# A last product in seven block products, accumulated in halves of PSUM banks, and its weights converted one stage later

## The chip, the cores and the metric

The kernel runs on one core of a Trainium2 chip. The time is device microseconds (us) of one execution. The engines are named as in the profile: PE is TensorE's matrix multiply and PEld its weight loads, DVE is VectorE, ACT is ScalarE, POOL is GpSimd, and SP is the queue that issues nearly all DMAs here.

## What is computed

The reference is a chain: windowed attention, then two stacks of matrix products. Cut to what matters:

```python
x = attention(q, k, v)                      # 4 x 8 heads x 576 x 64, window 64 -> x: 2304 x 512
a = x @ w1; b = x @ w2                      # 512 -> 1024
x = (a * b) @ w3 @ w_out                    # 1024 -> 1024 -> 512, "y" in the kernel
h = x @ w_in                                # 512 -> 2048
g = np.maximum(0.01 * h, h)                 # leaky relu
out = g @ w_out2                            # 2048 -> 512, float32
```

The weights arrive as 64-bit floats and are handed over as 64-bit integers; the kernel makes 32-bit floats of their words itself.

## The kernel before

Every large product is done three times on PE: each operand is split into a high and a low part in a rounded 32-bit type, and `mm3` (lines 74 to 77) issues high by high, high by low and low by high. Lines L75, L76 and L77 of the profile are these three matmuls, whatever stage they belong to; a stage is known by the tile's name.

The stages follow each other:

- **w3 with w_out** are multiplied into one matrix `wf` while the weights land (tiles `mm<-w,w3T`), together with the first batch's attention.
- **x to y**, four batches of 16 steps. `ab_step` multiplies x by w1 and w2 (tiles `ab`, 288 columns), `y_step` multiplies the product by `wf` (tiles `mm`, 288 columns). The next batch's attention is laid between (`sc` are its scores, `pa` its second product, which takes `pts`, loaded back from a DRAM tile `pd`). Here too the words of w_in (16 units) and w_out2 (16 units) are converted: `advance` (lines 284 to 314) takes a unit of 128 by 512 values that a DMA has landed in `raw`, scales the high words on ACT (L293, `f`), takes three bits of the low words on ACT (L295, `low`), shifts and joins them on DVE (L310) and sets the sign on DVE (L306); `keep` stores the result to the DRAM tile `wd`. The loads of units wait, by an order edge, for the last entry of `pss["store"]`, which `tp` sets to the store of `pd`. One call of `advance` is made per step, from step 4 of the second batch on (line 692).
- **y to h** is done in seven block products instead of eight: y and w_in are cut in quarters, `y_parts` and `w_parts` form sums of quarters and split them, and a `Quad` (p, c) multiplies the seven pairs for 256 of the 2048 columns (p, 0 to 7) and 768 of the 2304 rows (c, 0 to 2): tiles `pr`, 384 columns, 42 matmuls in a quad. ACT copies products out of PSUM (L640) and DVE adds others to them (L643), in the order that `Quad.ORDER` gives; the result `c` goes to the DRAM tile `hd`. `at_slot` lays the preparation of operands to slots, and a slot is one of the seven products (6 matmuls).
- **h to out**, the last stage, is a plain product: for each chunk c of 384 rows and each f of 16 blocks of 128 columns, `load_h` fetches a piece of h, `split_h` makes the leaky relu (ACT L748 and DVE L749) and the two parts (ACT L750 and DVE L751), and `o_step` multiplies three blocks of 128 rows by 128 rows of w_out2 (tiles `o`, 512 columns; 9 matmuls to a step). The rows of w_out2 come back from `wd` and are split by `store` (L259 and L260). One PSUM bank holds one block of 128 rows until all 16 steps have been added.

Of the kernel before, what the change touches and what calls it, by code (L numbers as in the profile page):

```python
# [21 lines left out]
def tile_kernel(ctx: ExitStack, tc: tile.TileContext, q, k, v, w1, w2, w3, w_out, w_in, w_out2, out):  # L22
# [184 lines left out]
    def tp(g):  # L207
# [75 lines left out]

    def advance(stop):

        now = dict(n_of)
        if now["scale"] < min(stop, now["load"]):
            u = units[now["scale"]]
            w = flat(u["raw"]).bitcast(I32).rearrange("p (m two) -> p m two", two=2)
            u["hi"] = w[:, :, 1]  # L290
            u["f"] = stage.tile([P, UC], F32, name="f", tag="f", bufs=4)
            with tc.issue_after(pss["copy"]) if now["scale"] >= PHASE_B else nullcontext():
                act.mul(u["f"], u["hi"].bitcast(F32), 2.0 ** -112)  # L293
                u["low"] = stage.tile([P, UC], I32, name="low", tag="low", bufs=1)
                act.activation(out=u["low"], in_=flat(u["raw"]).bitcast(U8).rearrange("p (m e) -> p m e", e=8)[:, :, 3],  # L295
                               func=AF.Copy, scale=1.0 / 32, bias=-31.0 / 64)
# [10 lines left out]
        if now["shift"] < now["scale"]:  # L307
            u2 = units[now["shift"]]
            g = u2["f"].bitcast(I32)
            dve.scalar_tensor_tensor(out=g, in0=g, scalar=3, in1=u2["low"], op0=ALU.logical_shift_left, op1=ALU.bitwise_or)  # L310
            n_of["shift"] += 1
        if d:
            n_of["bits"] += 1
# [70 lines left out]
    for f in range(KF2):  # L384
        unit(w_out2[P * f:P * f + P, :], keep(KF2 + f), ("wo2", f))
    n_of["cap"] = len(units)
# [181 lines left out]
    def w_parts(p):  # L568
# [4 lines left out]
        def part(j):  # L573
            u = win[p]
            a11, a21, a12, a22 = u[0][:, :, 0], u[0][:, :, 1], u[1][:, :, 0], u[1][:, :, 1]
            if j == 1:
                if p:
                    both = stage.tile([P, 2, 2, 2, P], F32, name="raw", tag="raw", bufs=RAW)
                    own["sums"] = [both[:, 0], both[:, 1]]
                else:  # L580
                    own["sums"] = [stage.tile([P, 2, 2, P], F32, name="io", tag="io", bufs=2) for _ in range(2)]
# [306 lines left out]
```

## Time and profile before

| what | value |
|---|---|
| median of 3 runs | 868.76 us (868.71 to 870.02) |
| profiled execution, its own time | 870.25 us |
| its span, first to last instruction | 868.5 us |
| PE busy in the span | 820.0 us (94%) |
| DVE, ACT busy | 513.9 us (59%), 438.8 us (51%) |
| last stage, first to last matmul of `o` | 662 to 862 us |

The profiled execution has 1.75 us around its span. PE's busy time counts modelled ends of pipelined matmuls; the distance from one matmul's start to the next says more than a matmul's duration.

### The profile page before, as it was taken

The page shows a single profiled execution, that of the slowest core. Times are in us where ns is not written, and L with a number is a line of the kernel's source. Part 1 is how long each engine was busy: PE and PEld are TensorE (multiplying, and loading weights), DVE is VectorE, ACT ScalarE, POOL GpSimd, SP SyncE. Part 2 cuts the span into 40 slices and gives each one's busy share as a digit, 9 for nine tenths or more (in the row PEclk, how much of TensorE's full clock was granted, in tenths as well). Part 3 has the DMA queues.
Part 4 walks back from the last instruction along what each step waited for, and adds up shares of the span by engine and source line. Part 5 has one row for each costly group of instructions (what it writes and reads, how often), then busy time and mean ns, then how long its engine had stood idle before and what let it go on. Part 6 is the DMA issues. An engine that isn't in the chain of part 4 may idle for free.

```text
span 868.5 us, 15320 instructions
## 1 busy us (share of the span) xinstructions
PE 820.0 (94%) x5332; PEld 754.7 (87%) x5332; DVE 513.9 (59%) x1307; ACT 438.8 (51%) x1091; POOL 66.7 (8%) x77
## 2 busy tenths in 40 slices
PE   5788798999999899899999999999998999999997
PEld 4567698989999899899999999999997888888885
DVE  6897996563676567564821864433338555555552
ACT  6676983432555365454521654333336555455552
POOL 1012543110111001110000000000000000000000
PEclk9999999999999999999999999999999999999999
DMA  7797787664688888875610355333239335344341
GB/s 249 197 209 205 203 212 199 140 152 88 162 216 215 213 251 220 234 240 160 184 46 1 128 188 193 133 134 135 105 121 290 102 98 166 94 134 130 99 129 45
DMA packets 203694, 139.44 MB, mean 161 GB/s; under 512 B 137312, under 2 KB 181856, under 8 KB 203616
## 3 DMA queue, kind: packets, MB, share of 16 engines
q1 hardware_dynamic: 199008, 133.74, 54.2%
q10 hardware_dynamic: 4608, 4.72, 1.6%
q8 instruction: 42, 0.69, 0.3%
q14 instruction: 36, 0.29, 0.1%
HBM read 94.63 MB, written 43.78 MB: 159 GB/s over the span
## 4 chain that ended last, share of the span: by engine, by line
PE 73%; DMA 12%; ACT 5%; DVE 4%; SPq 3%; issue 2%; POOL 1%; ACTq 0%; DVEq 0%; POOLq 0%
PE o L75 8%; PE o L76 8%; PE o L77 8%; PE pr L75 6%; PE pr L77 6%; PE pr L76 6%; PE ab L75 6%; PE ab L77 6%; DMA raw<-in_moe_w_dram 6%; PE ab L76 6%; PE mm L75 3%; PE mm L77 3%; PE mm L76 3%; DMA pts<-pd 2%; PE sc L175 2%
## 5 line engine op out<-in xcount | busy, mean ns | idle before, releaser
L75 PE MATMUL ab<-x,w 128*128 128x288 f32 x512 | 154.6, 302 | 6.1 <-ACT x L235 3.3
L77 PE MATMUL ab<-x,w 128*128 128x288 f32 x512 | 152.5, 298 | 0.0
L76 PE MATMUL ab<-x,w 128*128 128x288 f32 x512 | 152.3, 298 | 0.0
L75 PE MATMUL o<-w,g 128*128 128x512 f32 x288 | 113.2, 393 | 2.9 <-DVE c L643 2.9
L76 PE MATMUL o<-w,g 128*128 128x512 f32 x288 | 113.1, 393 | 0.0
L75 PE MATMUL pr<-yop,w 128*128 128x384 f32 x324 | 109.3, 337 | 1.4 <-ACT c L640 1.4
L77 PE MATMUL pr<-yop,w 128*128 128x384 f32 x324 | 109.1, 337 | 0.0
L76 PE MATMUL pr<-yop,w 128*128 128x384 f32 x324 | 109.0, 336 | 0.0
L75 PEld LDWEIGHTS ab<-x,w 128*128 128x128 f32 x512 | 97.7, 191 | 7.8 <-ACT x L235 3.5
L77 PEld LDWEIGHTS ab<-x,w 128*128 128x128 f32 x512 | 97.4, 190 | 0.1
L76 PEld LDWEIGHTS ab<-x,w 128*128 128x128 f32 x512 | 97.4, 190 | 0.1
L640 ACT COPY c<-pr 128x384 f32<-128x384 f32 x95 | 45.6, 480 | 94.5 <-PE pr L77 89.8
L643 DVE TENSOR_TENSOR c<-pr,c 128x384 f32<-128x384 f32 x74 | 41.1, 556 | 78.2 <-PE pr L77 59.6
L77 PE MATMUL o<-w,g 128*128 128x512 f32 x288 | 82.8, 393 | 0.0
L749 DVE TENSOR_TENSOR t<-h,t 128x384 f32<-128x384 f32 x96 | 53.5, 557 | 48.5 <-ACT t L748 48.4
L748 ACT ACTIVATE t<-h 128x384 f32<-128x384 f32 x96 | 50.4, 525 | 53.2 <-DVE g L751 52.5
L75 PE MATMUL mm<-ab,wf 128*128 128x288 f32 x256 | 76.8, 312 | 0.0
L77 PE MATMUL mm<-ab,wf 128*128 128x288 f32 x256 | 74.8, 294 | 0.0
L76 PE MATMUL mm<-ab,wf 128*128 128x288 f32 x256 | 74.4, 293 | 0.0
L751 DVE TENSOR_TENSOR g<-t,g 128x384 fp32r<-128x384 f32 x96 | 53.4, 557 | 29.7 <-ACT g L750 29.2
L183 ACT ACTIVATE s<-s,nm 128x128 f32<-128x128 f32 x144 | 56.5, 396 | 24.0 <-DVE nm L179 23.6
L75 PEld LDWEIGHTS o<-w,g 128*128 128x128 f32 x288 | 54.1, 188 | 15.4 <-DVE c L643 3.3
(94 smaller groups left out, 1560.8 us busy)
## 6 DMA issues: line engine op xcount, KB each, us to landing
hd<-c SPq DMA_DIRECT2D x96, 192.0 KB, 1.9
h<-hd SPq DMA_DIRECT2D x96, 192.0 KB, 2.4
raw<-in_moe_w_dram SPq DMA_DIRECT2D x32, 512.0 KB, 4.8
raw<-in_moe_w_out_dram SPq DMA_DIRECT2D x24, 512.0 KB, 4.5
raw<-in_moe_w_in_dram SPq DMA_DIRECT2D x16, 512.0 KB, 5.3
wd<-f SPq DMA_DIRECT2D x32, 256.0 KB, 4.1
vt<-in_v_dram SPq DMA_DIRECT2D x56, 128.0 KB, 2.7
pd<-tb SPq DMA_DIRECT2D x36, 192.0 KB, 2.3
```

The source lines that it names most:

```text
L75: pe.matmul(ps, lhsT=lh, rhs=rh, start=first, stop=False, skip_group_check=more)
L76: pe.matmul(ps, lhsT=lh, rhs=rl, start=False, stop=False, skip_group_check=more)
L77: return pe.matmul(ps, lhsT=ll, rhs=rh, start=False, stop=last, skip_group_check=more).ins
L175: pe.matmul(sc[:, t, :], lhsT=qb[:, t, :], rhs=kT[n][:, k0:k0 + P], start=True, stop=True)
L183: act.activation(out=s[:, t, :], in_=s[:, t, :], func=AF.Exp, bias=nm[:, t:t + 1], scale=-1.0, accum_out=sm[:, t:t + 1])
L640: pss["copy"] = act.copy(self.sb[to], ps).ins
L643: pss["add"] = dve.tensor_tensor(out=self.sb[to], in0=self.ps[at], in1=self.sb[of or to], op=ALU.add).ins
L748: act.mul(t, h, 0.01)
L749: dve.tensor_tensor(out=t, in0=h, in1=t, op=ALU.max)
L751: dve.tensor_tensor(out=g[:, 1], in0=t, in1=f32(g[:, 0]), op=ALU.subtract)
```

## The change

The last stage becomes seven block products too. The names w_out2's operands now go by are `v_load`, `v_parts` and `vop`; those of h are `h_load`, `h_sums`, `h_split` and `g_units`. A group is 512 rows (four groups, and a last one of 256), and k is one of 8 blocks of 256 columns of h. A step (group, k) has two `o_quad`s of 21 matmuls of 256 columns (one in the last group). All 8 steps of a group add into the same PSUM tiles: `BANKS` gives the products of one quad as four banks, two products to a bank in its halves, except one. After step 7 `o_out` adds the seven products to the four quarters of the result. The leaky relu is one ACT instruction (L814), in place on 128 by 1024 values. The last three p of y to h now run c by c, so that the operands of y come free earlier, and the first operands of the last stage are made in their room.

w_out2's words are converted beside y to h (`c_load`, `c_scale`, `c_shift`, `c_sign`, at slots 38 to 122), and only w_in's in the batches, from step 4 of the third batch on. For these the ACT instruction for `low` is gone: DVE shifts and masks, and joins the three bits straight from the low word in one instruction more. `pss["store"]` is now the last load of `pts`. The operands of w_in are one tile of seven for each p. The diff, cut to its core:

```diff
@@ tp, advance
-        pss["store"] = sp.dma_start(pd, tb).ins
+        sp.dma_start(pd, tb)
...
-            sp.dma_start(pts[32 * b:32 * b + 32], pd[:, b].rearrange("(a j) t i -> j a (t i)", a=4))
+            pss["store"] = sp.dma_start(pts[32 * b:32 * b + 32], pd[:, b].rearrange("(a j) t i -> j a (t i)", a=4)).ins
...
+                if now["scale"] < PHASE_B:
+                    low_bits(u)
...
+            if "low" in u2:
+                dve.scalar_tensor_tensor(out=g, in0=g, scalar=3, in1=u2["low"], op0=ALU.logical_shift_left, op1=ALU.bitwise_or)
+            else:
+                dve.tensor_scalar(g, g, 3, 0x7FFFFFF8, op0=ALU.logical_shift_left, op1=ALU.bitwise_and)
...
+            if "low" not in u:
+                dve.scalar_tensor_tensor(out=f, in0=u["lo"], scalar=29, in1=f, op0=ALU.logical_shift_right, op1=ALU.bitwise_or)
...
-            if 2 * KF * b + s >= 2 * KF * (B - 3) + 4:
-                advance(len(units))
+            if 2 * KF * b + s >= 2 * KF * (B - 2) + 4:
+                advance(KEPT)
@@ last stage
-    def o_step(c, f):
-        g = g_t.pop((c, f))
-        w = rows2(slots["wo2", f // 2])
-        for tb in range(TB):
-            if f == 0:
-                po[c, tb] = ps3.tile([P, DM], F32, name="o")
-            ts = slice(P * tb, P * tb + P)
-            mm3(po[c, tb], g[:, 0, ts], g[:, 1, ts], w[:, 0, f % 2, :], w[:, 1, f % 2, :], f == 0, f == KF2 - 1)
...
+    BANKS = ((1, 2), (6, 7), (4, 5), (3,))
...
+            for at, x in (((0, u[:, 0, 0:1]), (1, u[:, 1])), ((3, own.get("sums", (0,))[0]),), ((5, own.get("sums", (0, 0))[-1]),))[j]:
+                w = slice(at, at + x.shape[1])
+                act.copy(t[:, 0, w], x)
+                dve.tensor_tensor(out=t[:, 1, w], in0=x, in1=f32(t[:, 0, w]), op=ALU.subtract)
...
+            act.activation(out=x, in_=x, func=AF.Prelu, alpha=0.01)
+            x = hin[i] = x.rearrange("p f (t m) -> p (f t) m", t=2)
+            t13, t24 = hsum[i] = [stage.tile([P, 2, width(i)], F32, name="f", tag="f", bufs=4) for _ in range(2)]
+            dve.tensor_tensor(out=t13, in0=x[:, 1:4:2], in1=x[:, 0:2], op=ALU.subtract)
+            dve.tensor_tensor(out=t24[:, 0], in0=x[:, 3], in1=t13[:, 0], op=ALU.subtract)
+            dve.tensor_tensor(out=t24[:, 1], in0=x[:, 2], in1=t24[:, 0], op=ALU.subtract)
...
+            for at, y in ((0, x[:, 0:1]), (1, x[:, 2:4]), (3, t13), (5, t24)):
+                h, l = (u[:, n, at:at + y.shape[1], 0:width(i)] for n in range(2))
+                act.copy(h, y)
+                dve.tensor_tensor(out=l, in0=y, in1=f32(h), op=ALU.subtract)
...
+        if k == 0:
+            po[g, q] = [ps3.tile([P, 2, 2 * P], F32, name="o") for _ in BANKS]
+        for bank, ms in enumerate(BANKS):
+            for n, m in enumerate(ms):
+                a, b = O_PRODUCTS[m]
+                with tc.issue_after(pss["pr"]):
+                    pss["pr"] = mm3(po[g, q][bank][:, n], y[:, 0, b, ts], y[:, 1, b, ts], w[:, 0, a], w[:, 1, a],
+                                    k == 0 and n == 0, k == NF - 1, True)
...
+        act.copy(own, m1)
+        add(res[:, 0, lo], m2, own)
+        add(u2, m6, own)
+        add(u3, m7, u2)
+        add(u2, m45[:, 1], u2)
+        add(res[:, :, hi], m45, u3.unsqueeze(1).to_broadcast([P, 2, 2 * P]))
...
+        add(res[:, 1, lo], m3, u2)
...
-    order = [(p, c) for c in range(NP) for p in range(FIRST)] + [(p, c) for p in range(FIRST, NF) for c in range(NP)]
+    LAST_P = range(NF - 3, NF)
+    order = ([(p, c) for c in range(NP) for p in range(FIRST)] + [(p, c) for p in range(FIRST, NF - 3) for c in range(NP)]
+             + [(p, c) for c in range(NP) for p in LAST_P])
...
+    for f in range(KF2):
+        t0 = 38 + 5 * f
+        for n, g in ((0, c_load), (7, c_scale), (8, c_shift), (9, c_sign)):
+            at_slot(t0 + n, lambda f=f, g=g: g(f))
...
+        h_load(i + 4)
+        h_sums(i + 3)
+        for q in range(width(i) // P):
+            o_quad(i, q)
+        h_split(i + 2)
+        if i < len(later):
+            if i % 2 == 0 and i:
+                v_load(5 + i // 2)
+            run(later[i])
```

`later` holds the parts of `v_parts` for k = 5, 6 and 7; those for k = 0 to 4 are laid to slots of y to h.

How the instructions stand on PE where y to h ends and the last stage begins (`pr` is a product of y to h, `o` of the last stage; `yop` is y's or, in the last stage, the room of y's operands). Before:

```order
3559 L77 MATMUL pr<-yop_6577,w_7623 128x384
3560 L75 MATMUL o<-w_7897,g 128x512
3561 L76 MATMUL o<-w_7897,g 128x512
3562 L77 MATMUL o<-w_7897,g 128x512
3563 L75 MATMUL o<-w_7897,g 128x512
```

With the change:

```order
3559 L77 MATMUL pr<-yop_6414,w 128x384
3560 L75 MATMUL o<-yop 128x256
3561 L76 MATMUL o<-yop 128x256
3562 L77 MATMUL o<-yop 128x256
3563 L75 MATMUL o<-yop 128x256
```

The matmuls of the last stage start at the same place, have half the columns, and read both operands from the room of y's operands.

DVE early in the last stage. Before, the leaky relu's maximum (L749) and the split (L751) alternate, and nothing else stands there:

```order
1030 L749 TENSOR_TENSOR t<-h,t 128x384
1031 L751 TENSOR_TENSOR g<-t,g 128x384
1032 L749 TENSOR_TENSOR t<-h,t 128x384
1033 L751 TENSOR_TENSOR g<-t,g 128x384
```

With the change, in the first group (L817 to L819 are `h_sums`, L829 `h_split`, L788 and L792 `v_parts`; `yop`, `yop_7863` and `yop_8080` are now rooms of the last stage's operands):

```order
1129 L817 TENSOR_TENSOR f<-raw 128x512
1130 L829 TENSOR_TENSOR yop_7863<-raw,yop_7863 128x512
1131 L788 TENSOR_TENSOR io<-raw 128x256 x2
1132 L792 TENSOR_TENSOR yop_8080<-raw,yop_8080 128x256
1133 L792 TENSOR_TENSOR yop_8080<-raw,yop_8080 128x512
1134 L818 TENSOR_TENSOR f<-raw,f 128x256
1135 L788 TENSOR_TENSOR io<-io,raw 128x256
1136 L829 TENSOR_TENSOR yop_8080<-raw,yop_8080 128x256
1137 L829 TENSOR_TENSOR yop_8080<-f,yop_8080 128x512
1138 L819 TENSOR_TENSOR f<-raw,f 128x256
1139 L788 TENSOR_TENSOR io<-raw,io 128x256
```

The sums and splits of h and those of w_out2 are woven into each other on one queue.

SP in the second batch of x to y, where loads of attention and of units share the queue. Before:

```order
162 L279 DMA raw<-in_moe_w_in_dram 128x2x256 x2
163 L378 DMA wd<-f 128x512
164 L151 DMA qin<-in_q_dram 32x18x32 x4
165 L216 DMA pts<-pd 32x4x96 x4
166 L213 DMA pd<-tb 128x384
167 L279 DMA raw<-in_moe_w_in_dram 128x2x256
```

With the change, at such a place:

```order
143 L151 DMA kin<-in_k_dram 32x18x32 x4
144 L213 DMA pd<-tb 128x384
145 L216 DMA pts<-pd 32x4x96 x4
146 L151 DMA vt<-in_v_dram 128x4x64 x4
147 L213 DMA pd<-tb 128x384
148 L151 DMA qin<-in_q_dram 32x18x32 x3
```

The loads and stores of units are gone from the second batch; those of w_in stand in the third and fourth.

## Rows read from the trace of the kernel before

**Rows 1.** The page: PE's granted clock in 40 equal slices, tenths of full speed.
```profile
PEclk9999999999999999999999999999999999999999
```

**Rows 2.** Busy time and matmuls of each stage: three batches of x to y, y to h, last stage.
```profile
core 0: us, PE busy (x) PEld busy (x) DVE busy (x) ACT busy (x) POOL busy (x), PEclk, DMA share, GB/s
...
150.00:233.00 83.00, 81.60 (x711) 78.65 (x710) 46.21 (x177) 33.44 (x124) 9.94 (x12) 1.00 0.55 126
233.00:316.00 83.00, 79.29 (x671) 76.50 (x670) 52.62 (x171) 41.70 (x124) 7.53 (x9) 0.98 0.83 221
316.00:399.00 83.00, 79.99 (x688) 77.32 (x688) 53.14 (x182) 44.54 (x140) 9.25 (x11) 1.00 0.82 232
...
482.00:662.00 180.00, 176.30 (x1005) 175.34 (x1003) 92.48 (x184) 79.59 (x170) 0.00 (x0) 1.00 0.46 156
662.00:862.00 200.00, 199.34 (x864) 162.37 (x864) 110.69 (x200) 104.00 (x204) 0.00 (x0) 1.00 0.40 119
```

**Rows 3.** The same view in stretches where PE has matmuls of 288, 384, 512 columns alone.
```profile
450.00:482.00 32.00, 32.00 (x242) 32.00 (x241) 6.00 (x14) 6.54 (x17) 0.00 (x0) 1.00 0.04 11
500.00:640.00 140.00, 140.00 (x802) 140.00 (x801) 61.69 (x123) 53.61 (x113) 0.00 (x0) 1.00 0.42 146
702.00:730.00 28.00, 28.00 (x121) 22.55 (x120) 15.20 (x29) 15.38 (x30) 0.00 (x0) 1.00 0.40 117
```

**Rows 4.** 128-column matmuls of PE: durations (min/median/max ns), then timeline (start, us).
```profile
L175 PE MATMUL sc<-kT,qbd x30: 271/275/377, 211.0 to 234.6; 128*128 128x128 f32 x30
...
216.38 0.83 PE L175 MATMUL sc<-kT,qbd 128*128 128x128 f32 x6
```

**Rows 5.** Groups by line with shapes: weight loads of the last stage, then ACT's conversions.
```profile
L75 PEld LDWEIGHTS o<-w,g 128*128 128x128 f32 x288 | 54.1, 188 | 15.4 <-DVE c L643 3.3
...
L293 ACT ACTIVATE f<-raw 128x512 f32<-128x512 f32 x72 | 48.8, 677 | 25.5 <-DMA raw<-in_moe_w_dram 18.1 <-DMA raw<-in_moe_w_out_dram 3.5 <-DMA raw<-in_moe_w_in_dram 1.7
...
L589 ACT CAST w<-raw 128x512 fp32r<-128x512 f32 x21 | 12.8, 622 | 0.1
...
L589 ACT CAST w<-raw 128x256 fp32r<-128x256 f32 x7 | 2.9, 409 | 0.6 <-ACT io L514 0.6
```

**Rows 6.** Timeline of DVE at the start of y to h, one behind the other.
```profile
485.80 0.42 DVE L590 TENSOR_TENSOR w<-raw,w 128x256 fp32r<-128x256 f32 x1
486.13 0.88 DVE L585 TENSOR_TENSOR raw<-raw 128x256 f32<-128x256 f32 x2
486.93 0.68 DVE L590 TENSOR_TENSOR w<-raw,w 128x512 fp32r<-128x512 f32 x1
487.53 1.02 DVE L546 TENSOR_TENSOR yop<-f,yop 128x384 fp32r<-128x384 f32 x2
```

**Rows 7.** Wait of PE from 640 to 664 us: total, times, longest.
```profile
PE o L75 <- DVE c L643: 2.9, 1, 2.9
```

**Rows 8.** Chain of work that ended last, 285 to 305 us: start, us, what.
```profile
293.42 2.27 SPq L151
...
297.80 1.95 DMA pts<-pd
...
301.40 0.24 PE ab L76
...
304.00 0.13 PE mm L77
```

**Rows 9.** Timeline of the tail: DVE's last copies: start, us, what, idle time before.
```profile
862.05 0.75 DVE L770 COPY io<-o 128x256 f32<-128x256 f32 x2 [5.16 <-ACT io L769]
865.06 0.42 DVE L770 COPY io<-o 128x256 f32<-128x256 f32 x1 [2.26 <-ACT io L769]
```

**Rows 10.** Timeline of DVE in the last stage, with its waits for ACT.
```profile
700.39 0.56 DVE L751 TENSOR_TENSOR g<-t,g 128x384 fp32r<-128x384 f32 x1 [0.40 <-ACT g L750]
701.54 0.56 DVE L749 TENSOR_TENSOR t<-h,t 128x384 f32<-128x384 f32 x1 [0.59 <-ACT t L748]
```

**Rows 11.** A DMA group: queue, count, KB of each, median us to landing.
```profile
raw<-in_moe_w_out_dram SPq DMA_DIRECT2D x24, 512.0 KB, 4.5
```

More of the change, by code (lines that the diff above doesn't have):

```diff
@@ L383, in tile_kernel @@
                  keep(2 * p + h), ("win", p, h))
-    for f in range(KF2):
-        unit(w_out2[P * f:P * f + P, :], keep(KF2 + f), ("wo2", f))
-    n_of["cap"] = len(units)
+    n_of["cap"] = KEPT = len(units)
     for name, p in [("wo", i) for i in range(4)] + [(n, p) for p in range(2) for n in ("w1", "w2")] + [("wf", i) for i in range(4)]:
@@ L576, in part @@
             if j == 1:
[L577 to L581, printed above, removed]
+                own["sums"] = [stage.tile([P, 2, 2, P], F32, name="io", tag="io", bufs=2) for _ in range(2)]
             if j in (1, 2):
@@ L661, in step @@
                     self.add("c21", "b")
+                if m == 5:
+                    self.sb["c12"] = self.sb["c22"]
+                    self.room("c22")
+                    self.add("c22", "b", "c12")
+                    self.out("c22")
                 if m == 4:
@@ new lines, in tile_kernel, with c_load, c_scale @@
+    BANKS = ((1, 2), (6, 7), (4, 5), (3,))
+    GTOK = 512
+    GROUPS = [(t0, min(GTOK, T - t0)) for t0 in range(0, T, GTOK)]
+    steps = [(g, k) for g in range(len(GROUPS)) for k in range(NF)]
+    conv = {}
+    def c_load(f):
+        u = conv[f] = {"raw": stage.tile([P, UC], I64, name="raw", tag="raw", bufs=RAW)}
+        sp.dma_start(u["raw"], w_out2[P * f:P * f + P, :])
+    def c_scale(f):
+        u = conv[f]
+        u["hi"] = u["raw"].bitcast(I32).rearrange("p (m two) -> p m two", two=2)[:, :, 1]
+        u["f"] = stage.tile([P, UC], F32, name="f", tag="f", bufs=4)
+        act.mul(u["f"], u["hi"].bitcast(F32), 2.0 ** -112)
+        low_bits(u)
@@ L838, in tile_kernel @@
             done += 1
[L839 to L848 removed]
+    while done <= max(todo, default=0):
+        prepare(done)
+        done += 1
+    yw.release()
     ps2.release()
     ps_h.release()
[L851 removed]
+    po_out = tc.alloc_tile_pool(name="po_out", bufs=2, side="right", reuse_waits="tile")
     ps3 = tc.alloc_tile_pool(name="ps3", bufs=8, space=PSUM, reuse_waits="tile")
[L853 to L856 removed]
+    later = []
+    for k, tile in ((5, w_unit), (6, next_unit), (7, next_unit)):
+        a, b, c = v_parts(k, tile)
+        later += [(a,), (b, c)]
+    h_load(2)
+    v_load(5)
+    h_load(3)
+    for i in range(len(steps)):
+        if i == 0:
+            three(ph, "yop2")
+            g_units.append(spare.pop())
+            h_sums(2)
+        h_load(i + 4)
[7 more added lines that the diff above has]
+            run(later[i])
+    for p in (ps3, po_out, yb0, ph, stage):
         p.release()
```

202 lines of the change are left out of this document (116 added, 86 removed).

## The prediction

> **What bounds the kernel now.** I read the granted clock first: full speed in all 40 slices, the stretch of rows 8 being too short to show there [rows 1]. Then the busy times by stage [rows 2]. The reader is to see that PE is the bound in all of them: in y to h it is busy 176.3 of 180 us, in the last stage 199.3 of 200, while DVE is busy 110.7 and ACT 104.0 there. So a stage's time is its number of matmuls times the distance between their starts. That distance comes from stretches with one width alone [rows 3]: 32 us / 242 = 132 ns at 288 columns, 140 / 802 = 175 at 384, 28 / 121 = 231 at 512. The matmuls last longer than that, but overlap.
>
> Where PE is not full: batches two and three of x to y (79.3 and 80.0 of 83 us against 81.6 in the first, which converts no units [rows 2]), 2.9 us at the start of the last stage, where PE waits for an add of DVE [rows 7], and the tail. In batch two one case can be followed in the chain [rows 8]: SP takes 2.27 us to issue an attention load, the `pts` loads come behind it, and after the wait PE's 288-column matmuls are 0.24 us apart instead of 0.13 from about 300 to 303 us. The granted clock of 0.98 in this batch [rows 2] says that this is the lower of its two levels, 1.2 instead of 2.4 GHz, after PE had stood idle.
>
> **The last stage, by PE.** Before: 864 matmuls of 512 columns, 200.0 us [rows 2]. After: 9 quads of 128 rows, 8 k, 7 products, 3 matmuls each: 1512 of 256 columns. The trace has no such width. A straight line through 288 and 512 columns gives 132 - 32 x (231 - 132) / 224 = 118 ns [rows 3]. Bounds: from above the 288-column row, 132; from below the 128-column row [rows 4], six in 0.83 us of which the last takes 0.275 itself, so (0.83 - 0.275) / 5 = 111. I take 118, since 256 is next to 288 and the rows up to 512 lie on one line. 1512 x 118 = 178.4 us: **-21.6 us** (-32.2 at 111, -0.4 at 132).
>
> Weight loads go from 864 to 1512, and one lasts 188 ns [rows 5]. That doesn't add up to 284 us, because loads overlap: in the 288-column stretch 241 of them are done in 32.0 us, one in 133 ns [rows 3], and at 128 columns load and matmul together take 111 [rows 4].
>
> The Trainium skill, Perfetto Trace Analysis, "Identifying the Most-Contended Engine", judges TensorE's headroom by the busy share of LDWEIGHTS rather than by that of matmuls; by that this change would be bound by loads and lose. The 288-column stretch speaks against it: loads are busy all of it, at 133 ns each, and PE keeps its pace. The skill, TensorE: Matmul & The Clock Gate, "Back-to-back issue gap", gives N / 2.4 + 2.5 ns, an estimate of 109 ns for 256 columns, and with it 165 us for the stage, 13.6 less than my term; but at 288 and 512 columns it gives 122.5 and 216, and this trace has 132 and 231.
>
> **The last stage, by DVE and ACT.** From one start to the next DVE takes 0.33 us for 256 elements and 0.60 for 512 [rows 6]. A step has `h_sums` 0.60 + 2 x 0.33 and `h_split` 0.33 + 3 x 0.60: 3.39 us, while PE takes 42 x 0.118 = 4.96. `o_out` is 5 x 0.33 + 0.60 = 2.25 a quad. A group: 8 x 3.39 + 2 x 2.25 = 31.6 against PE's 39.6. The first group also makes w_out2's operands for three k (4 x 0.33 + 0.33 + 3 x 0.60 = 3.45 each): 42.0, which is 2.4 more than PE. ACT: L814 on 1024 elements isn't in the trace; two L293 of 512, 1.35 us, bound it from above [rows 5], and I take that. With casts of 0.41 + 3 x 0.62 [rows 5] a step has 3.6 us, which is less than PE's, so the leaky relu costs nothing; without PE's 4.96 over it, it would cost the 1.35.
>
> Splits run two steps ahead, 9.9 us, which covers the 2.4 if the two queues keep busy. `o_out` frees banks one by one while the other quad's 21 matmuls (2.5 us) run; its chain takes about as long. I take **+3 us** for both (0 to +8).
>
> **Conversion beside y to h.** 16 units, each 2 x 0.67 us of ACT [rows 5] and, at DVE's 0.60, 1.2 of DVE: 21 and 19 us, under 180 us in which ACT is busy 79.6 and DVE 92.5 [rows 2]. SP gets 16 loads of 512 KB, landing in 4.5 us [rows 11], and 16 stores; the 12.6 MB in some 95 us come to 130 GB/s on top of 156, near 290, more than the 221 and 232 of batches two and three [rows 2]. Behind them on SP wait the stores of `hd`, which hold the buffers `c`, and for those ACT's copies and then PE. Toward its end the stage also makes the first operands of the last stage: five k of w_out2 (17 us of DVE) and two steps of h (7 us). I take **+1.5 us** (0 to +6).
>
> **Batches.** Batch two loses its units: it goes from 79.3 to the first batch's 81.6 busy us, 2.3, and the stretch at half clock is gone, about 14 matmuls x 0.11 = 1.5 [rows 2, 8]. Batch three keeps 16 units, with one DVE instruction more and one ACT instruction less on each (9.6 us of DVE on 53.1 of 83 busy), and `pts` ahead of a unit's load; I give it +0.3. **-3.5 us** (-5.5 to +2).
>
> **Start and tail of the last stage.** The first quad still needs banks that DVE's last adds free, with a full DVE queue: 2.9 us as now, **0** (-2.9 to +3). At the end the last copy of DVE ends at 865.48 and the span at 868.5 [rows 9]: 3.0 us for the store. After the last matmul there will be one add of 512 (0.68), one of 256 (0.42) and some 0.4 until they begin, then the 3.0: 4.5 instead of 6.5, **-1.9 us** (-3 to +1).
>
> **Sum**, against the profiled execution's 870.25 us: -21.6 + 3 + 1.5 - 3.5 + 0 - 1.9 = -22.5, so 847.75. The median of the runs is 1.5 below that execution (868.76), so 846.
>
> **Rivals.**
> *DVE and ACT take turns.* Today DVE waits 0.40 and 0.59 us for ACT at each instruction [rows 10]. In a step of the changed kernel five DVE instructions follow directly on ACT (L817, four L829). Without waits DVE has 4 x 31.6 + 3 x 3.45 for w_out2's operands + 17.8 for the last group (0.2 us for 128 elements, an estimate from rows 6) = 154.6 us. With five places in each of 40 steps it reaches PE's 178 at 0.12 us of waiting a place and today's 200 at 0.23. At 0.44 a place: 243 us, +43 and without my +3: 870.25 + 43 - 3.9 = 909, **908** as a median. At 0.17, partly the bound: 189 us, **854**. For it: the stage's queues are full of such pairs. Against it: today's waits are those of a queue that is idle half the time (110.7 of 200), and in rows 6 DVE follows ACT's casts without a gap. 0.05 for slower, 0.14 for partly.
>
> *A 256-column matmul takes as long as one of 288.* Weight loads, or something that doesn't shrink with columns, hold it at 132: 199.6 us, and the change doesn't do what it is built to: -0.4 - 0.9 = -1.3, **867.5**. For it: loads are busy without a break already at 288 columns [rows 3]. Against it: 111 at 128 columns. 0.05.
>
> *Loads don't overlap at this pace*: 188 ns each, 284 us, +84: **949**. Against it: rows 3 and 4 show 133 and 111. 0.01. It is what the rule of the Trainium skill, Perfetto Trace Analysis, would have here.
>
> *The lower bound holds*: 111 ns, 167.8 us: **836**. 0.06, since no row of a dense stretch is on it. The Trainium skill's 109 ns (TensorE: Matmul & The Clock Gate, above) would lie here.
>
> **How the numbers follow.** My case has 0.69; its own range is 838 to 853, from 114 to 122 ns and the smaller terms. Partly DVE reaches to 860. The range 835 to 860 leaves out the slower cases (0.11), a third of the fast one and the edges, together about 0.18. A measurement of this kernel tells about 0.2%, 1.7 us, from no change. Faster 0.88 (my case, partly DVE, the fast one, little of the 132 ns); same 0.05 (the 132 ns); slower 0.07 (0.05 + 0.01, and some of the 132 ns).
>
> **What would show it.** Distance between starts of `o` matmuls: 118 in dense stretches, 132 for the second rival. PE idle in the last stage under 6 us, and most of it in its first group; if DVE or ACT is the bound, PE waits for L829 in every group. PE busy near 81.6 in batch two without a stretch at half clock. DVE busy in y to h up by 19 us and more, PE's waits there under 5 us. I am wrong if `o` matmuls lie over 125 ns apart with PE dense, or if PE stands over 10 us in the last stage or at conversions beside y to h.

## The result, and the profile after

The changed kernel takes 857.9 us (856.19 to 859.36, four runs), the kernel before 868.84 beside it: a ratio of 0.987, interval 0.985 to 0.9891. It is faster, by 10.9 us where 22.8 were forecast. The profiled execution took 859.36 us, with a span of 857.6.

The page of the changed kernel (section 1, and the granted clock in tenths) answers to the table of before: PE's busy time fell by 13.4 us, DVE's rose from 513.9.

```profile
span 857.6 us, 16756 instructions
PE 806.6 (94%) x5980; PEld 774.5 (90%) x5980; DVE 583.9 (68%) x1505; ACT 446.6 (52%) x1095; POOL 66.4 (8%) x77
...
PEclk9999999999999999999999999999999999999999
```

Busy times of the changed kernel by stretch, columns as in [rows 2]: batches one to three, y to h, the last stage, and then pieces of the last stage.

```profile
150.00:233.00 83.00, 82.06 (x721) 79.04 (x720) 45.47 (x173) 30.97 (x117) 9.92 (x12) 1.00 0.55 129
233.00:316.00 83.00, 83.00 (x706) 80.69 (x706) 43.52 (x160) 30.82 (x112) 8.42 (x11) 1.00 0.47 111
316.00:399.00 83.00, 77.52 (x672) 74.20 (x672) 54.28 (x172) 33.93 (x111) 8.44 (x10) 1.00 0.69 186
482.00:657.00 175.00, 172.51 (x976) 171.52 (x974) 123.21 (x249) 98.89 (x204) 0.00 (x0) 0.99 0.70 233
657.00:852.00 195.00, 186.45 (x1509) 183.48 (x1508) 156.06 (x347) 115.10 (x212) 0.00 (x0) 0.98 0.38 119
...
657.90:670.00 12.10, 9.41 (x64) 9.21 (x65) 9.18 (x20) 7.24 (x13) 0.00 (x0) 0.86 0.47 144
670.00:698.00 28.00, 28.00 (x238) 28.00 (x237) 27.38 (x58) 20.36 (x38) 0.00 (x0) 1.00 0.47 147
698.00:718.00 20.00, 16.01 (x113) 15.06 (x113) 17.47 (x39) 11.89 (x20) 0.00 (x0) 0.91 0.42 138
...
800.00:853.00 53.00, 52.84 (x444) 52.63 (x442) 36.85 (x98) 25.56 (x61) 0.00 (x0) 1.00 0.23 70
```

The reader is to see three things. Batch two has lost its idle time (83.0 of 83), batch three has gained some (77.5 against 80.0). The last stage, where PE was busy 199.3 of 200 us, now has 8.6 us in which PE is idle, and a granted clock of 0.86 and 0.91 in the two stretches where that happens: a part of each ran at the lower level, 1.2 GHz. And DVE is busy 27.38 of 28 us just between them, in the first group of 512 rows.

PE's waits in the changed kernel, by what it waited for (total, times, longest, us): in the last stage, then in y to h.

```profile
PE o L75 <- DVE res L858: 3.5, 4, 1.5
PE o L75 <- DVE c L651: 3.3, 2, 2.6
PE o L75 <- DVE c L858: 1.5, 2, 0.9
...
PE pr L77 <- DVE w L598: 2.5, 2, 2.1
```

L651 is the add of y to h whose result frees a PSUM bank for the first quad; L858 is the add of `o_out` that frees one for the next group.

To see where the time went I read the stages' lengths off PE's timeline: from the first matmul of a stage to the first of the next, `o` from its first to its last matmul, the tail from there on, `w3` from ACT's first instruction, b1 to b4 the batches. In brackets is the time at the lower clock, up to the last matmul. The experiments are listed too; e11 is the kernel before once more.

```
               w3           b1           b2          b3          b4         pr          o            tail
before         102.9(10.2)  104.1(6.8)   97.4(3.4)   96.6        79.5       181.4       199.0        6.8
e11_before     103.3(10.2)  100.1(3.4)   100.8(6.8)  96.8        79.5       182.0(0.3)  200.5(3.1)   6.8
after          101.9(6.8)   102.8(6.8)   92.5        98.8        79.4       181.8(3.4)  194.6(6.8)   5.0
e1_start       102.3(13.7)  101.5(6.8)   92.5        100.6(3.4)  79.4       179.7       192.3(6.8)   5.0
e2_order       102.0(13.7)  99.9(3.4)    92.5        101.2(5.8)  79.9(1.0)  181.2(3.4)  188.5(6.8)   5.0
e3_pool        103.7(10.2)  102.7(10.2)  92.5        100.2(5.0)  80.3(1.9)  181.9(3.4)  200.4(10.2)  5.4
e4_all         102.0(13.7)  100.0(3.4)   92.5        103.9(5.2)  80.2(1.6)  181.4(3.4)  193.2(6.8)   5.0
e5_lows        101.9(10.2)  101.7(6.8)   92.5        99.9        79.4       181.3(3.4)  184.0        5.0
e6_sums        102.1(17.1)  99.9(3.4)    92.5        101.6(5.6)  80.0(1.2)  177.6       186.9(3.4)   5.0
e7_cols        101.2(10.2)  103.5(6.8)   92.5        101.4(3.4)  79.7       179.8       181.4(6.8)   5.1
e8_early       102.3(6.8)   100.5(3.4)   99.3(3.4)   93.7        79.7       182.0(3.4)  195.3(10.2)  5.0
e9_spread      103.7(10.2)  101.2(6.8)   92.5        92.6        79.7       177.6       186.7(3.4)   5.0
e10_edge       101.2(6.8)   102.3(6.8)   92.5        92.6        79.5       177.6       187.9(6.8)   5.0
e12_edge_alone 101.4(6.8)   102.0(3.4)   92.5        93.4        79.4       180.3       195.0(6.8)   5.0
e13_both       99.5(6.8)    101.7(3.4)   92.5        92.6        79.5       177.6       187.3(3.4)   5.0
```

b1 differs by 4 us between the two executions of the kernel before, so a microsecond or two in it says nothing; b2 differs by 3.4 and the last stage by 1.5, each with more time at the lower clock in the longer one.

### The profile page after: what moved, and what is told of

Its sections match the earlier page's. It is cut to its first block, busy times and chain, and to the rows that moved or that the text cites. A ratio compares the mean times of both kernels' runs of the same rounds, so it can differ in the third digit from the quotient of the medians.

```text
span 857.6 us, 16756 instructions
## 1 busy us (share of the span) xinstructions
PE 806.6 (94%) x5980; PEld 774.5 (90%) x5980; DVE 583.9 (68%) x1505; ACT 446.6 (52%) x1095; POOL 66.4 (8%) x77
## 4 chain that ended last, share of the span: by engine, by line
PE 72%; DMA 10%; DVE 9%; ACT 3%; SPq 2%; issue 2%; POOL 0%; DVEq 0%; ACTq 0%; POOLq 0%
PE o L75 7%; PE o L77 7%; PE o L76 7%; PE ab L75 7%; PE ab L77 6%; PE ab L76 6%; PE pr L77 6%; PE pr L75 6%; PE pr L76 6%; PE mm L75 4%; DMA raw<-in_moe_w_dram 4%; PE mm L76 4%; PE mm L77 3%; PE sc L175 3%; PE pa L229 2%
## 5 line engine op out<-in xcount | busy, mean ns | idle before, releaser
L77 PE MATMUL pr<-yop,w 128*128 128x384 f32 x300 | 102.0, 340 | 2.5 <-DVE w L598 2.5
L75 PE MATMUL pr<-yop,w 128*128 128x384 f32 x300 | 101.7, 339 | 0.0
L76 PE MATMUL pr<-yop,w 128*128 128x384 f32 x300 | 101.5, 338 | 0.0
L75 PE MATMUL o<-yop,yop 128*128 128x256 f32 x259 | 74.4, 287 | 4.7 <-DVE res L858 3.0
L77 PE MATMUL o<-yop,yop 128*128 128x256 f32 x259 | 73.6, 284 | 0.0
L76 PE MATMUL o<-yop,yop 128*128 128x256 f32 x259 | 73.5, 284 | 0.0
L502 DVE TENSOR_TENSOR p<-ab,a 128x288 f32<-128x288 f32 x64 | 28.9, 452 | 60.5 <-PE ab L77 59.9
L651 DVE TENSOR_TENSOR c<-pr,c 128x384 f32<-128x384 f32 x74 | 41.1, 556 | 38.7 <-PE pr L77 22.0
L497 ACT COPY a<-ab 128x288 f32<-128x288 f32 x64 | 25.4, 398 | 77.9 <-PE ab L77 75.4
L829 DVE TENSOR_TENSOR yop<-f,yop 128x512 fp32r<-128x512 f32 (+1 forms) x80 | 48.7, 636 | 25.0 <-ACT yop L828 23.8
L192 POOL TENSOR_TENSOR s<-s,rs 128x384 f32<-128x384 f32 x48 | 41.3, 861 | 297.1 <-DVE rs L191 200.9
```

The costliest lines, as they stand in the source:

```text
L75: pe.matmul(ps, lhsT=lh, rhs=rh, start=first, stop=False, skip_group_check=more)
L76: pe.matmul(ps, lhsT=lh, rhs=rl, start=False, stop=False, skip_group_check=more)
L77: return pe.matmul(ps, lhsT=ll, rhs=rh, start=False, stop=last, skip_group_check=more).ins
L192: pool.tensor_tensor(out=s, in0=s, in1=rs.unsqueeze(2).to_broadcast([P, GT, P]), op=ALU.mult)
L497: pss["copy"] = act.copy(pss["a"], ps).ins
L502: dve.tensor_tensor(out=p32, in0=ps, in1=pss["a"], op=ALU.mult)
```

## What the experiments had to tell apart

In the last stage the starts of `o` matmuls lie 0.12 us apart in dense stretches (a step of 42 takes 5.03 to 5.04 us, every third or so 4.93). 1512 of them are 181.4 us, and the stage has 194.6. What a step takes beyond 0.12 a matmul, by (group, step): (0,0) 4.5 us; (0,7), (1,0) and (1,1) together 6.7; (2,0) 1.65; (3,0) 1.55; the others are 1.1 us under it in all.

**Theory: DVE's queue**, in two ways. Its *order*: adds that free banks stand behind `h_sums` and `h_split`, at the stage's start and at each change of group. And its *amount*: in the first group it has more to do than PE. **Rivals:** DVE and ACT take turns (a rival of the prediction); weight loads or a floor per matmul rather than DVE set the pace. For the batches: it is the order edge that was moved, or it is the amount of conversion in batch three. For y to h: SP's queue and bandwidth, or a buffer.

## Experiments in the last stage

Each ratio is against runs of the kernel before on the same chip.

**e1_start**: the sums of two steps of h are put behind the last adds of y to h.

```diff
-            h_sums(2)
+            with tc.issue_after(pss["add"]):
+                h_sums(2)
...
-        h_sums(i + 3)
+        with tc.issue_after(pss["add"]):
+            h_sums(i + 3)
```

> Edit: the sums of h for steps 2 and 3 are issued behind the last add of y to h, no work left out. Theory A (PE's losses in the last stage are waits for PSUM banks, because the adds that free them stand behind other instructions on DVE's queue): the wait at the second bank of the first quad (2.65 us) and the half clock behind it (some 1.7 us) go, 3 to 4.5 us faster than the changed kernel, about 854. Rival B (DVE has too much work, or takes turns with ACT, so what is put off is late elsewhere): under 1 us gained, PE waits as long for splits in the first group.

The timeline of DVE in the changed kernel, at the stage's start, shows what it undoes (start, us, what, idle time before and its releaser):

```profile
657.33 1.02 DVE L651 TENSOR_TENSOR c<-pr,c 128x384 f32<-128x384 f32 x2
658.26 0.43 DVE L818 TENSOR_TENSOR f<-raw,f 128x256 f32<-128x256 f32 x1
660.40 0.69 DVE L817 TENSOR_TENSOR f<-raw 128x512 f32<-128x512 f32 x1 [1.71 <-ACT raw L814]
661.01 0.42 DVE L788 TENSOR_TENSOR io<-raw,io 128x256 f32<-128x256 f32 x1
661.35 0.42 DVE L829 TENSOR_TENSOR yop<-raw,yop 128x256 fp32r<-128x256 f32 x1
661.68 0.55 DVE L651 TENSOR_TENSOR c<-pr,c 128x384 f32<-128x384 f32 x1
```

And ACT's, for the instruction that L817 waits for:

```profile
659.32 1.06 ACT L814 ACTIVATE raw<-raw 128x1024 f32<-128x1024 f32 x1 [3.58 <-DMA raw<-hd]
```

The last L651 frees the bank that PE needs. It stands behind an L817, which waits for the leaky relu, which waits for a load of h. Measured: 855.84 us, ratio 0.9819 (0.9782 to 0.9855). Step (0,0) went from 4.5 to 0, but (0,7) from 1.7 to 7.8: over the first group and its end 8.75 us are lost instead of 11.2. The start is order; it hides an amount that comes due at the end of the group.

**e2_order**: in addition the adds of `o_out` set `pss["add"]`, and `h_split(i + 2)` is issued behind it too.

```diff
-            dve.tensor_tensor(out=out, in0=ps, in1=x, op=ALU.add)
+            pss["add"] = dve.tensor_tensor(out=out, in0=ps, in1=x, op=ALU.add).ins
...
-        h_split(i + 2)
+        with tc.issue_after(pss["add"]):
+            h_split(i + 2)
```

> Edit: as the run on the start, and in the last step of each group the splits of h are issued behind the adds that free the banks; no work left out. A: beside the start, the starts of groups 2 and 3 lose under 0.5 us each instead of 1.6, and the first boundary about half of its 6.7 us; 7 to 9 us faster than the changed kernel, about 850. B: the splits become late instead, PE waits for L829 in each group, no better than the run on the start alone.

In the changed kernel the adds are woven into the splits; this is DVE's timeline at the change from the second group to the third. The twelve adds of the two quads (L858) take from 747.13 to 755.48, 8.3 us, of which 4.5 are their own; PE waits until 753.60 for the one that begins at 753.13:

```profile
747.13 0.42 DVE L858 TENSOR_TENSOR res<-o,c 128x256 f32<-128x256 f32 x1
...
750.40 0.68 DVE L858 TENSOR_TENSOR res<-o,c 128x512 f32<-128x512 f32 x1
750.99 0.68 DVE L829 TENSOR_TENSOR yop<-f,yop 128x512 fp32r<-128x512 f32 x1
751.59 0.42 DVE L858 TENSOR_TENSOR c<-o,c 128x256 f32<-128x256 f32 x1
751.93 0.68 DVE L829 TENSOR_TENSOR yop<-raw,yop 128x512 fp32r<-128x512 f32 x1
752.53 0.68 DVE L817 TENSOR_TENSOR f<-raw 128x512 f32<-128x512 f32 x1
753.13 0.42 DVE L858 TENSOR_TENSOR res<-o,c 128x256 f32<-128x256 f32 x1
...
755.06 0.42 DVE L858 TENSOR_TENSOR res<-o,c 128x256 f32<-128x256 f32 x1
```

Measured: 851.77 us, 0.976 (0.9722 to 0.9797). The losses at (2,0) and (3,0) are gone, the stage is 188.5 us. What stays is in the first group, 1.4 at (0,2) and 6.1 at (0,7); PE waits there for operands (L792, L829, L791) and no longer for L858. Busy times of e2_order in that group:

```profile
667.00:677.00 10.00, 8.82 (x75) 8.62 (x74) 10.00 (x23) 7.54 (x15) 0.00 (x0) 1.00 0.49 157
677.00:687.00 10.00, 10.00 (x86) 10.00 (x85) 10.00 (x22) 7.60 (x13) 0.00 (x0) 1.00 0.57 162
687.00:697.00 10.00, 8.48 (x70) 8.07 (x68) 9.97 (x22) 8.38 (x16) 0.00 (x0) 1.00 0.41 114
697.00:707.00 10.00, 8.79 (x49) 8.53 (x50) 7.99 (x19) 5.69 (x10) 0.00 (x0) 0.66 0.41 153
```

DVE is busy without a gap for 30 us, PE stands at the end of them, and its clock is 0.66 in the next 10. Before that DVE had stood once, for 2.15 us: the cast that it waits for is behind a leaky relu in ACT's queue, and that one waits for a load of h (DVE, then ACT, of e2_order):

```profile
661.37 1.22 DVE L829 TENSOR_TENSOR yop<-raw,yop 128x256 fp32r<-128x256 f32 x2 [2.15 <-ACT yop L828]
```

```profile
659.98 1.06 ACT L814 ACTIVATE raw<-raw 128x1024 f32<-128x1024 f32 x1 [4.17 <-DMA raw<-hd]
```

A queue that took turns with ACT would have gaps all along; in the changed kernel DVE waits for L828 only 1.8 us in two places between 657 and 700.

**e5_lows**: e2_order without the subtractions for the low parts of k = 5 to 7 (3 x 2.13 us less for DVE); k = 0's low parts are read there instead, by an edit in `o_quad` that is not shown.

```diff
-                dve.tensor_tensor(out=t[:, 1, w], in0=x, in1=f32(t[:, 0, w]), op=ALU.subtract)
+                if k < 5:
+                    dve.tensor_tensor(out=t[:, 1, w], in0=x, in1=f32(t[:, 0, w]), op=ALU.subtract)
```

> Edit: on the run on the order, the low parts of w_out2's operands for k = 5 to 7 are left out (those of k = 0 are multiplied in their place): 6.4 us less of DVE in the first group, nothing given to POOL. Theory A' (the first group is bound by the amount of DVE's work: 8 steps, three k of w_out2, the fourth that isn't done when the stage begins, and o_out, some 46 us against PE's 40): the first group's 7.5 us over its 42 x 8 matmuls fall under 2, 5 to 6 us faster than the run on the order, about 846. Rival B (ACT and DVE take turns, or loads of h come late for want of raw buffers): the casts and loads are all still there, 0 to 2 us gained.

Measured: 846.84 us, 0.9718 (0.9676 to 0.976). The stage falls to 184.0 us and has no time at the lower clock. In its first group:

```profile
677.00:687.00 10.00, 10.00 (x86) 10.00 (x85) 8.46 (x19) 7.69 (x15) 0.00 (x0) 1.00 0.35 108
687.00:697.00 10.00, 10.00 (x87) 10.00 (x86) 7.28 (x16) 7.47 (x14) 0.00 (x0) 1.00 0.49 159
```

Less work for DVE, and PE is dense: it was the amount. What the stage still loses, 3.3 us in (0,7), (1,0) and (1,1), is waiting for adds of `o_out` at the end of the first group.

**e3_pool** gives the same subtractions to POOL, on the changed kernel; **e4_all** does so on e2_order.

```diff
-                dve.tensor_tensor(out=t[:, 1, w], in0=x, in1=f32(t[:, 0, w]), op=ALU.subtract)
+                (pool if k >= 5 else dve).tensor_tensor(out=t[:, 1, w], in0=x, in1=f32(t[:, 0, w]), op=ALU.subtract)
```

> Edit: the low parts of w_out2's operands for k = 5 to 7 are subtracted on POOL instead of DVE, 6.4 us less of DVE in the first group; no work left out. A with DVE behind in the first group alone: the first boundary loses 1.6 us like the others, not 6.7, so 4 to 5 us faster than the changed kernel, about 853. B by turns with ACT: the number of pairs that alternate on DVE's queue is hardly less, gain under 2 us.

> Edit: the three edits together, no work left out. A: the last stage comes down to its 1512 matmuls at 0.12 us, 181.4 us, and 1 to 2 us; 11 to 12 us faster than the changed kernel, about 846. B: over 852, with PE waiting for splits.

Measured: 864.8 us, 0.9916 (0.9887 to 0.9944), and 859.3, 0.9838 (0.9799 to 0.9877): the last stage is 5.8 and 4.7 us longer than without POOL, not shorter. The cause is in two timelines of e3_pool, of POOL and then of DVE:

```profile
683.89 1.47 POOL L792 TENSOR_TENSOR yop<-raw,yop 128x512 fp32r<-128x512 f32 x1 [0.30 <-ACT yop L791]
687.58 1.43 POOL L792 TENSOR_TENSOR yop<-io,yop 128x512 fp32r<-128x512 f32 x1 [2.22 <-ACT yop L791]
```

```profile
684.13 1.77 DVE L817 TENSOR_TENSOR f<-raw 128x512 f32<-128x512 f32 x1
...
687.77 1.52 DVE L819 TENSOR_TENSOR f<-raw,f 128x256 f32<-128x256 f32 x1
```

L817 takes 1.77 instead of 0.68 us and ends 0.54 after POOL's instruction; L819 takes 1.52 instead of 0.42 and ends 0.28 after it. So DVE, with two inputs in SBUF, stood until POOL was nearly done. It is so with all twelve instructions that POOL got: the DVE instruction under way at POOL's end ended 0.28 us (256 elements) or 0.55 us (512) behind it. In all DVE's took 9.7 us longer beside them, where 6.4 us of its work had gone. POOL took more from the bottleneck than it did for it. (DVE held POOL up as well: in e4_all one of POOL's took 4.85 us, while DVE ran eight in a row.)

**e7_cols**: e2_order with 192 columns in the matmuls of k > 0.

```diff
+                    c = 2 * P if k == 0 else 192
-                    pss["pr"] = mm3(po[g, q][bank][:, n], y[:, 0, b, ts], y[:, 1, b, ts], w[:, 0, a], w[:, 1, a],
+                    pss["pr"] = mm3(po[g, q][bank][:, n, 0:c], y[:, 0, b, ts], y[:, 1, b, ts], w[:, 0, a, 0:c], w[:, 1, a, 0:c],
```

> Edit: on the run on the order, all o matmuls but those of k = 0 multiply 192 of 256 columns (a quarter of the last stage's columns is left out). If columns set the distance of 120 ns at 256: 90 ns at 192 in stretches where PE is dense, or PE waits for DVE all the time. If something with a floor sets it (a weight load, one for each matmul): 110 to 120 ns at 192 too.

One run, 847.21 us, of a kernel that leaves out a quarter of the columns of k > 0. A stretch of it with 192-column matmuls alone:

```profile
715.00:743.00 28.00, 28.00 (x254) 28.00 (x252) 21.30 (x44) 20.30 (x35) 0.00 (x0) 1.00 0.39 114
```

28.00 / 254 = 110 ns, and 112 from start to start (a step of 42 takes 4.69 us), where 90 would be in proportion to 120 at 256 columns. There is a floor near 112, and 256 columns lie just above it. What makes the floor isn't shown; the 128-column row of before, 111 [rows 4], lies on it too. This run also bears on DVE's amount: PE's part of the first group fell from 40.3 to 37.9 us, and the group takes 47.9 us against 47.7 in e2_order. So in the first group DVE sets the time, not PE.

## Experiments in y to h and in the batches

**e6_sums**: e2_order with the sums of w_in's quarters for p = 1 and 2 in `raw`, as in the kernel before. That they had moved to the two `io` buffers is a part of the change that the diff above, cut to its core, doesn't show.

```diff
-                own["sums"] = [stage.tile([P, 2, 2, P], F32, name="io", tag="io", bufs=2) for _ in range(2)]
+                if 0 < p < 3:
+                    both = stage.tile([P, 2, 2, 2, P], F32, name="raw", tag="raw", bufs=RAW)
+                    own["sums"] = [both[:, 0], both[:, 1]]
+                else:
+                    own["sums"] = [stage.tile([P, 2, 2, P], F32, name="io", tag="io", bufs=2) for _ in range(2)]
```

> Edit: on the run on the order, the sums of w_in for p = 1 and 2 go to a raw buffer again, as before the change, instead of the two io buffers; no work left out. If PE's wait of 2.1 us early in y to h and the half clock behind it come from parts of w that wait for those two buffers: the wait goes, 2 to 4 us faster than the run on the order, about 849. If DVE is simply full there (y's operands and w's at once): the wait stays, no difference over 1 us.

Measured: 847.48 us, 0.9718 (0.9678 to 0.9759). PE's wait for L598 and the 3.4 us at the lower clock behind it are gone, and y to h goes from 181.2 to 177.6 us with every conversion still in it. PE is dense there, with DVE busy 118.8 of 170 us:

```profile
480.00:650.00 170.00, 170.00 (x972) 170.00 (x973) 118.79 (x239) 98.01 (x206) 0.00 (x0) 1.00 0.71 235
```

**e8_early**: the changed kernel with w_in's units from step 4 of the second batch on.

```diff
-            if 2 * KF * b + s >= 2 * KF * (B - 2) + 4:
+            if 2 * KF * b + s >= 2 * KF * (B - 3) + 4:
```

> Edit: the changed kernel with the units of w_in converted from step 4 of the second batch again, as before the change; no work left out. If the 4 us gained in the batches are the second batch without units: half to all of it comes back, PE's busy share of the second batch falls from near full, +1 to +3 us on the changed kernel. If it is the order edge on the loads of pts, or the missing low instruction of ACT: no difference over 1 us in the batches.

Measured: 855.94 us, 0.983 (0.9793 to 0.9867), on a chip whose own before was 870.42. Batch two is 99.3 instead of 92.5, batch three 93.7 instead of 98.8: with the moved edge the units cost 5 to 7 us where they stand. The two together are 1.7 us longer, as expected; the whole kernel is not slower, its ratio being 0.983 against 0.987.

**e9_spread**: e6_sums with a unit at every second step of the third batch. **e10_edge**: e6_sums with the order edge put back on the store of `pd`. **e12_edge_alone**: the changed kernel with that edge alone. **e13_both**: e9_spread with that edge.

```diff
@@ e9_spread, e13_both
-            if 2 * KF * b + s >= 2 * KF * (B - 2) + 4:
+            if 2 * KF * b + s >= 2 * KF * (B - 2) + 4 and (b == B - 1 or s % 2 == 0):
@@ e10_edge, e12_edge_alone, e13_both
-        sp.dma_start(pd, tb)
+        pss["store"] = sp.dma_start(pd, tb).ins
...
-            pss["store"] = sp.dma_start(pts[32 * b:32 * b + 32], pd[:, b].rearrange("(a j) t i -> j a (t i)", a=4)).ins
+            sp.dma_start(pts[32 * b:32 * b + 32], pd[:, b].rearrange("(a j) t i -> j a (t i)", a=4))
```

> Edit: on the run on the sums, units of w_in are advanced in every second step of the third batch and in every step of the fourth; no work left out. Theory C (16 units cost the batch that they lie in 4 to 8 us, wherever that is, since attention's DMAs and DVE work share their queues; the fourth batch has no attention and room): the third batch falls from some 101 to 97 us, the fourth stays at 80 to 81, 2 to 4 us faster than the run on the sums, about 844. Rival: the third batch's length comes from pts alone, no difference over 1 us; or the fourth batch's loads of y and w now wait for buffers and PE loses as much there.

> Edit: the run on the sums with the order edge of unit loads back on the store of pd instead of the last load of pts; no work left out. If the edge shortens the waits for pts: the third batch gets 1 to 3 us longer. If it does nothing: within 1 us, and the batches' lengths as before.

> The changed kernel with the order edge of the unit loads alone put back on the store of pd. If the moved edge is what takes batch three from the forecast +0.3 to +2.2 us, batch three goes from 98.8 us to 93 or less and PE no longer waits for pts nor behind L521 there; the last stage keeps its 194 to 195 us and its two half-clock stretches, since nothing in it is touched; the whole is near 0.992 of the changed kernel, about 851 us, a ratio to before of 0.979. If the gain in the earlier run with this edge came from its other edits (the sums of w_in's quarters in another buffer, the order of the last stage's splits), batch three stays at 98 to 101 us and the time at 858.

> The best version so far: sums in the other buffer, the last stage's order, the units at every second step in the third batch, and the edge back on the store. If the spread and the edge cure the same delay (a unit's load that lands late behind pts on SP, with ACT's copies for PE queued behind it), they do not add up: batch three stays at 92 to 93 us and the time at 838 to 841, a ratio of 0.960 to 0.963. If they are two delays, batch three falls further, below 91, and the time to 836 or less. In both cases the last stage stays at 186 to 188 us.

Measured: 839.46 us, 0.9615 (0.958 to 0.9649); 840.59, 0.9628 (0.9599 to 0.9656); 851.33, 0.9746 (0.9722 to 0.9771); 838.54, 0.9605 (0.9583 to 0.9627). Batch three is 92.6, 92.6, 93.4 and 92.6 us. (e12's profile is 7.8 us shorter than that of the changed kernel: 5.4 are batch three, 1.5 y to h, which had no time at the lower clock here, the rest w3 and b1.) I had expected 97 us of batch three in e9, and the old edge to make it 1 to 3 us longer in e10; it made it 9.0 shorter. And since the two edits together bring no more than either, they cure one delay. SP's timeline in the changed kernel shows it (L216 loads `pts`, L279 a unit):

```profile
347.34 0.40 SPq L279 DMA_DIRECT2D raw<-in_moe_w_in_dram  x1
...
348.30 0.42 SPq L213 DMA_DIRECT2D pd<-tb  x1
353.06 1.74 SPq L216 DMA_DIRECT2D pts<-pd  x4
354.90 2.05 SPq L151 DMA_DIRECT2D vt<-in_v_dram  x4
...
357.60 0.38 SPq L279 DMA_DIRECT2D raw<-in_moe_w_in_dram  x1
```

The `pts` loads wait on SP for the store of `pd` to land, until 353.06. In that batch (296 to 396 us) SP's waits of this kind come to 28.1 us, 11 times, 4.7 at most:

```profile
SPq L216 <- DMA pd<-tb: 28.1, 11, 4.7
```

With the moved edge the next unit comes behind them and is issued at 357.60. In e12_edge_alone it is issued ahead of them, at 346.87. ACT in the changed kernel:

```profile
363.30 0.66 ACT L298 ACTIVATE f<-raw 128x512 f32<-128x512 f32 x1 [3.91 <-DMA raw<-in_moe_w_in_dram]
363.86 0.38 ACT L521 COPY io<-mm 128x288 f32<-128x288 f32 x1
```

L298 waits 3.91 us for the unit. Behind it stands L521, the copy that frees a bank, and PE waits 2.06 us for that, the longest of its waits there. Another of 2.0 us is for `pts` itself (PE's waits from 290 to 400 us):

```profile
PE mm L75 <- ACT io L521: 2.1, 1, 2.1
PE pa L229 <- DMA pts<-pd: 2.0, 1, 2.0
```

In e12_edge_alone PE has neither.

The same stretch in e12_edge_alone, and then in the changed kernel:

```profile
306.00:399.00 93.00, 92.32 (x790) 89.50 (x790) 63.83 (x205) 42.00 (x136) 9.43 (x11) 1.00 0.70 197
```

```profile
306.00:399.00 93.00, 87.52 (x750) 84.20 (x749) 60.71 (x198) 39.10 (x130) 9.43 (x11) 1.00 0.67 181
```

**e11_before**, the kernel before once more:

> The kernel before, once more, for a second profile of it: how far the lengths of the batches and of the last stage stray from one execution to the next without any edit. Last stage within 0.5 us; the first two stages within some 3 us, since waits for DMAs and stretches at half clock fall otherwise.

872.33 us; the table above has its stages. The last stage was expected within 0.5 us and is 1.5 longer, with 3.1 us at the lower clock; b2 is 3.4 longer and b1 4.0 shorter, a little more than the 3 expected.

## Why the prediction was right in kind and wrong in size

The sum was -22.5 us against the profiled execution's 870.25. The two profiles give -10.9. By its terms:

- **The last stage, by PE**: forecast -21.6, measured 181.4 - 199.0 = -17.6. The same reading as in [rows 3] gives 28.00 / 238 = 118 ns, as forecast; but such a count has the two or three matmuls in it that are under way at the edge. From start to start it is 120, which makes 3.0 us. (Taken so, 288 and 512 columns lie 133 and 231 apart, and the line through them gives 119: the line held, the count was short.) The other 1.0 is the base: I took 200.0 us from a window for a stage of 199.0. That a 256-column matmul takes as long as one of 288 is refuted (120 against 133, both from start to start), and that 111 holds is too. Weight loads, busy 28.00 of 28 us, didn't bind by their length: one lasts 191 to 200 ns in this stage, and 237 were done in these 28 us. The Trainium skill, TensorE: Matmul & The Clock Gate, "Back-to-back issue gap", gives the formula behind the 109 ns for a matmul by itself, and for a stream of weight loads and matmuls about 81 ns at 128 columns and 131 at 512. The prediction used the formula without that distinction. These traces agree with neither: 111, 120 and 231 at 128, 256 and 512 columns.
- **The last stage, by DVE and ACT, and its start**: forecast +3 and 0, measured 13.2 us within the stage and 2.3 less ahead of it, together +10.9. This is the step that failed, twice. "Splits run two steps ahead, 9.9 us, which covers the 2.4 if the two queues keep busy" took the lead as there when the stage begins. It wasn't: `h_sums(2)` and the last 1.5 us of the operands of k = 4 were then still to be made [e2_order], so that DVE had 42.0 + 1.5 + 1.26 = 44.8 us to do against PE's 40.3, and was at 100% from 667 to 697 us. Nor did the queues keep busy: DVE stood 2.15 us near the start, for a cast behind a load of h that was late. e5_lows takes 6.4 us of work away and gets 4.5 of the stage back. How much of the loss the late load makes by itself wasn't tested. And "`o_out` frees banks one by one while the other quad's 21 matmuls (2.5 us) run" counted its own 2.25 us, not the splits that stand between its adds in the same queue; e2_order puts those behind, and the losses at the later groups go. The start, which I left as it was, grew for the same reason: an add stood behind an instruction that waited for a load. I had counted work on the queue, and not what stands ahead of the one instruction that PE needs. The clock added to it: 6.8 us at the lower level cost about half of that, 3.4.
- **DVE and ACT take turns**, the rival, is not it: DVE waits for L828 in the later groups, where it has time, and hardly in the first (1.8 of 27.1 us in the changed kernel's stage lie before 700 us).
- **Conversion beside y to h**: forecast +1.5, measured +2.7 from the first to the last `pr` (178.5 to 181.2). The size is near by luck, the reason another. It is no queue on SP, nor the 233 GB/s: PE waited for L598 alone, and e6_sums takes that away by another buffer. With that it is 177.6 us with them, so the conversions cost next to nothing, and DVE's 31 us more in that stage are hidden.
- **Batches**: forecast -3.5, measured -5.1 with w3; 2.3 of these are w3 and b1, which differ by as much without an edit. Batch two did as argued, 97.4 to 92.5 (100.8 in e11_before). Batch three I gave +0.3 for "`pts` ahead of a unit's load"; it was +2.2, and without the moved edge it would have been 93.4 - 96.6 = -3.2. The edge costs 5.4 us: I named it and priced SP's issue times, but not that `pts` waits on SP for a store to land, nor that ACT's copies for PE stand behind the scale of a late unit.
- **Tail**: forecast -1.9, measured -1.8. DVE's last two groups of the changed kernel, whose last matmul starts at 852.56 and ends at 852.84, against [rows 9]:

```profile
851.86 1.40 DVE L858 TENSOR_TENSOR c<-o,c 128x256 f32<-128x256 f32 x3
853.18 1.01 DVE L858 TENSOR_TENSOR res<-o,c 128x512 f32<-128x512 f32 x2
```

L814 took 1.06 us, under my bound of 1.35.

So of the 11.6 us that are missing 4.0 are PE's pace and its base, 7.9 DVE's queue in the last stage (10.9 - 3), 1.2 the conversions and 0.1 the tail, less 1.6 from the batches and w3. Undoing the queue's order, the buffer and the edge [e10_edge] gives 18.2 us back on profiles (859.36 to 841.17): 6.7 in the last stage, 4.2 in y to h, 6.2 in batch three, the rest in w3 and b1. What stays in the last stage is the first group's, some 6 us; a version that keeps all low parts and makes the operands of k = 4 and the loads of h earlier wasn't tried. What makes the floor near 112 ns is open.

## What to carry to other kernels

Before a queue's busy share is compared with the bottleneck's, look for the one instruction on it that the bottleneck needs next, and count what stands ahead of it, with the waits of those. When work moves to a stage with slack on average, count the first group apart: what must be made before it can run is added to what it makes for later. An order edge on a DMA queue moves everything behind it to where the edge's own waits end; its price is read from the waits of the transfers ahead, not from their issue times.

## What the runs showed of the hardware

- While POOL runs a two-input instruction on SBUF (1.4 to 1.5 us for 128x512), a DVE instruction with two inputs in SBUF stands until it is nearly done: 0.68 became 1.77 us, 0.42 became 1.52 [e3_pool]. The Trainium skill, SBUF — State Buffer, "SBUF: two separate sides", says that the pair of ports which the two share is a lock for a whole instruction; these rows agree.
- The distance between matmuls' starts, each with its own weight load, has a floor in these runs: 112 ns at 192 columns [e7_cols], 111 at 128 [rows 4], against 120 at 256 and 133 at 288.
- In the last stage of the changed kernel PE stood 2.6 us in the first step of the first group, and 1.5, 0.7, 0.9 and 0.9 us at the change to the second group, and both times a stretch at 1.2 GHz followed (granted clock 0.86 in 657.9 to 670 us, 0.91 in 698 to 718); 0.56 us at a later change of group was not followed by one. The same wait doesn't always bring it: of the nine runs with the 2.1 us wait for L598, six had 3.4 us at 1.2 GHz behind it and three (e1_start, e7_cols, e12_edge_alone) had none; and the 2.9 us at the start of the last stage had it in e11_before, not in the kernel before.
